# exp(c) of the last pair taken from exp(-c): a reciprocal on VectorE for one unit, a power of -1 on GpSimd for the other

## The chip, the core and the metric

One core of one Trainium2 chip runs the whole program. The metric is the device time of one execution in microseconds (us); less is better. The kernel before takes 178.74 us (median of two runs, 178.31 and 179.16).

## What is computed

A gated linear attention (4 batches, 8 heads, 768 steps, head size 48) feeds a two-layer network with a silu between:

```
f = 1 / (1 + exp(-f_logit))
for t in range(S):
    state = f[t] * state + outer(k[t], v[t])     # per batch and head, 48 x 48
    y[t]  = q[t] @ state
x   = y, heads side by side                       # 3072 tokens x 384
h   = x @ w_in                                    # 384 -> 2048
out = (h * sigmoid(h)) @ w_out                    # 2048 -> 384, float32
```

## The kernel before

The 768 steps of a batch are cut into chunks of 128. A unit is one chunk of one batch, with all 8 heads; two units make a pair, and 12 pairs make the program. Pairs 0 to 3 (form T) hold the first two chunks of one batch, pairs 4 to 11 (form N) the same chunk of two batches. Pair 10 is chunk 5 of batches 0 and 1, pair 11, the last, chunk 5 of batches 2 and 3. A unit is written (pair, place), so (11, 0) is batch 2 and (11, 1) batch 3; a step is written kind.pair.place.

The steps of a unit, with the lines that the profile shows for them:

- E and L (L229, L236; ScalarE): exp(-f) and ln(1 + that), the negative log of the gate. One pair's gates at a time.
- cs (L302; TensorE): running sum c of it over the chunk, by a triangular matrix, into PSUM.
- a and ia (both L307; ScalarE): a = exp(-c) and ia = exp(c), 128 x 384, from PSUM into buffers of the class x, of which there are five.
- qg and ki (both L312; VectorE or GpSimd): q * a and k * ia, into the two halves of a buffer qk.
- the transpose of qk: qkD (L327) is a transposing DMA that SyncE issues; it moves both halves at once, so it needs qg and ki.
- sc (L340; TensorE): scores; at (L344; VectorE): the mask, in two halves.
- vb (L180 on ScalarE, L182 on VectorE or GpSimd): v as bf16.
- y (L352 with the state of the chunk before, L356 with the masked scores and vb; TensorE), yc (a cast of y out of PSUM), and the transpose of y: yD (L368), a transposing DMA from SyncE, in the late pairs.
- d, sd, al, su (L373, L377, L309, L383): the state for the next chunk; su runs on GpSimd as two instructions.
- mi (L244; TensorE): 1st layer, eight steps of twelve matmuls a pair, over both units, so it needs both transposes of y; si (L249; ScalarE): silu; mo (L279; TensorE): 2nd layer; oc (L180 or L182): the copy out of PSUM; so (L287, L289): the store.

Nothing schedules at run time. A text, PLAN (lines 37 to 103), lists every step in one order, as `kind.pair.place:engine:slots`, with the engine (A ScalarE, V VectorE, G GpSimd, P TensorE, S SyncE) and the buffer slots. Each engine carries out its own steps strictly in that order and waits by semaphore for those of others. The loads (L223), the transposing DMAs and most stores are all issued by SyncE, in one queue. ScalarE has two sets of tables, one for exp and ln and one for silu; the program loads the other set (L473) at each turn from one kind to the other in PLAN. This is the stretch of it that the change touches (from lines 89 to 94, with the steps of TensorE, the masks but one entry and most steps of the two layers left out):

```
qg.10.1:G  q.11.0:S  qg.11.1:G  qg.10.0:V  so.7.1:S  sd.8.0:V
ia.11.1:A  a.11.0:A  qg.11.0:G  ia.11.0:A  qkD.10.1:S
ki.10.0:V  qkD.10.0:S  su.8.0:G  ki.11.0:G  oc.9.1:V  oc.9.0:A
v.10.0:S  v.11.0:S  ki.11.1:G  qkD.11.1:S  so.4.1:S
at.10.*:V  qkD.11.0:S  vb.10.1:A  vb.10.0:G  yD.10.1:S  yD.10.0:S
```

The step a.11.1 (exp(-c) of the other unit) stands earlier, on line 87. On TensorE the same stretch and what follows is: sc.10, the rest of mi.8, y.10.1, y.10.0, the last 28 matmuls of mo.8, sc.11, mi.10, y.11 and then mi, mo of pairs 10 and 11 to the end.

Of the kernel before, what the change touches and what calls it, by code (L numbers as in the profile page):

```python
# [10 lines left out]
F32 = mybir.dt.float32  # L11
# [18 lines left out]
    ('N', (0, 5), (1, 5)),  # L30
    ('N', (2, 5), (3, 5)),
]

SLOTS = dict(f=4, k=6, q=6, v=6, e=2, lf=3, x=5, qk=5, vb=7, qkT=4, qkTT=2, atm=4, yb=3, xT=4, hT=4, sd=2, al=6, ob=6, pb=8, st0=1, st1=1, st2=1, st3=1)

# [71 lines left out]
def kernel(  # L107
# [10 lines left out]
    nc = tc.nc  # L118
    B, H, S, D = q.shape
    C = 128  # L120
# [8 lines left out]
    sb = ctx.enter_context(tc.tile_pool(name="sb", bufs=1))  # L129
# [16 lines left out]
    triu = sb.tile([C, C], BF16, name="triu")  # L146
    ident = sb.tile([C, C], BF16, name="ident")
    ones = sb.tile([C, 1], BF16, name="ones")
    zero = sb.tile([C, 512], BF16, name="zero")
    two = any(kind == "T" for kind, *_ in PAIRS)  # L150
    if two:
# [11 lines left out]
    for word in PLAN.split():  # L163
        name, eng, got = word.split(":")
# [10 lines left out]
    at = lambda *key: where[key]  # L175
    ENG = {"A": nc.scalar, "V": nc.vector, "G": nc.gpsimd, "S": nc.sync}
# [20 lines left out]
    def emit(kind, rest, eng):  # L197
# [9 lines left out]
        P = rest[0]  # L207
# [65 lines left out]
        i = rest[1]  # L273
# [16 lines left out]
        elif kind == "cs":  # L290
            lf, cs = at("lf", P), at("cs", P, i)
            main = cs[:, 0:HD].rearrange("p (h d) -> p h d", d=D)
            if T:
                for j in range(2):
                    nc.tensor.matmul(main, tincl if j <= i else tstrict, lf[:, j, :, 0:D], start=(j == 0), stop=(j == 1), skip_group_check=True)  # L295
                if i == 1:
                    for p in range(NP):
                        for j in range(2):
                            nc.tensor.matmul(cs[:, HD + 2 * p:HD + 2 * p + 2], lf[:, j, 2 * p:2 * p + 2, :], halves,
                                             start=False, stop=(j == 1), skip_group_check=True)  # L300
            else:
                nc.tensor.matmul(main, triu, lf[:, i, :, 0:D], start=True, stop=True, skip_group_check=True)  # L302
                if not last:
                    for p in range(NP):
                        nc.tensor.matmul(cs[:, HD + p:HD + p + 1], lf[:, i, 2 * p:2 * p + 2, :], ones, start=False, stop=True, skip_group_check=True)
        elif kind in ("ia", "a"):
            nc.scalar.activation(at(kind, P, i).rearrange("p h d -> p (h d)"), at("cs", P, i)[:, 0:HD], AF.Exp, scale=1.0 if kind == "ia" else -1.0)  # L307
        elif kind == "al":
# [112 lines left out]
    def run(kind, rest, eng, got):  # L421
        if kind == "idle":
            for _ in range(rest[1]):
                nc.tensor.matmul(buf["pb", int(got)][:, 0:rest[0]], triu, zero[:, 0:rest[0]], start=True, stop=True, skip_group_check=True)  # L424
            return
        slots = iter(got.split(",") if got else [])
        for key in takes(kind, rest):
            if key not in where:
                cls = cls_of(key[0])
                if cls == "st":  # L430
                    cls = f"st{PAIRS[key[1]][1 + key[2]][0]}"
                elif cls == "qkT" and len(key) == 2:
                    cls = "qkTT"
                where[key] = buf[cls, int(next(slots))]
        assert next(slots, None) is None, (kind, rest, got)
        emit(kind, rest, eng)
# [4 lines left out]
    with tc.manual_schedule():  # L441
        nc.scalar.preload_act_table_set(TABLES["exp"])
        loads = [t for t in plan if t[0] in SRC][:4]
        for t in loads:
            run(*t)
        make_upper_triangular(nc, triu, 1.0, diag=True)
        nc.vector.memset(zero, 0.0)
        nc.vector.memset(ones, 1.0)
        if two:
            nc.gpsimd.memset(tincl, 0.0)  # L450
            nc.gpsimd.memset(tstrict, 0.0)
            for r in range(2):
                half = slice(r * HC, (r + 1) * HC)
                make_upper_triangular(nc, tincl[half, half], 1.0, diag=True)
                make_upper_triangular(nc, tstrict[half, half], 1.0, diag=False)
            nc.vector.memset(halves, 0.0)
            for r in range(2):
                nc.vector.memset(halves[r * HC:(r + 1) * HC, r:r + 1], 1.0)
        for cls in ("lf", "qk"):
            for s in range(SLOTS[cls]):  # L460
                nc.vector.memset(buf[cls, s][:, :, :, D:64], 0.0)
        make_identity(nc, ident)
        for b in range(B):
            nc.vector.memset(buf[f"st{b}", 0], 0.0)
        if two:
            for r in range(2):
                half = slice(r * HC, (r + 1) * HC)
                for j in range(2):
                    for t in range(2):
                        nc.vector.tensor_copy(masks[j][half, t * HC:(t + 1) * HC], (tincl if j <= t else tstrict)[half, half])  # L470
        for n, t in enumerate(plan):
            if n in turns:
                nc.scalar.preload_act_table_set(turns[n])  # L473
            if t not in loads:
                run(*t)
# [30 lines left out]
```

## Time and profile before

| | |
|---|---|
| median of two runs | 178.74 us |
| the profiled execution | 178.94 us |
| its span, first to last instruction | 177.2 us |
| granted TensorE clock, mean | 1.000 |
| ScalarE busy | 130.4 us (74%) |
| VectorE busy | 81.2 us (46%) |
| GpSimd busy | 62.5 us (35%) |

The profile is of one execution. PE is TensorE's matmuls, PEld its weight loads, DVE VectorE, ACT ScalarE, POOL GpSimd, SPq SyncE's queue. A timeline line reads: start, length, engine, line, operation, out<-in, count, and in brackets the idle time before it with what ended it; merged lines stand for several instructions in a row. The end of a matmul is modelled, so a line can overlap the next by some 0.17 us. The time from the issue of a DMA to its landing is counted from the start of the issue. Where an instruction waits for several things the profile names the one that ended last by its record, which need not be the one that it needed.

### The profile page before, as it was taken

Reading aid. Unit: us, or ns where it says so; the run is one execution under the profiler, and the core shown is the slowest. Engines: PE = TensorE matmul, PEld = TensorE weight load, DVE = VectorE, ACT = ScalarE, POOL = GpSimd, SP = SyncE. Lnnn points to the kernel's source line nnn. Section 1 sums busy time; section 2 is a strip of 40 time slices with the busy share of each in tenths; the row PEclk is TensorE's granted clock in tenths of the full one; section 3 lists DMA queues with packets and bytes.
Section 4 is the critical chain, followed back from the end, with each engine's and each line's share of the span. In section 5 each row is a group of like instructions: output and inputs, shape, how many; then the busy total and the mean of one; then the engine's idle time right before and its main releaser. Section 6 shows DMA issues by size and latency. Waiting matters only on the chain.

```text
span 177.2 us, 4721 instructions
## 1 busy us (share of the span) xinstructions
PE 170.6 (96%) x1912; PEld 124.7 (70%) x1915; DVE 81.2 (46%) x165; ACT 130.4 (74%) x241; POOL 62.5 (35%) x105
## 2 busy tenths in 40 slices
PE   6998999999999999999999999999999999999991
PEld 2446688666886788766787687686797686877860
DVE  7089751047795783125777174035770152520110
ACT  3968578953999989998499788899589574281721
POOL 6056593102383348400647323400471960000001
PEclk9999999999999999999999999999999999999999
DMA  5999999999999989997698796899968998132202
GB/s 145 301 311 256 213 225 204 188 179 237 218 196 201 211 177 199 219 204 151 135 231 152 148 228 141 213 192 212 234 129 191 212 150 242 48 91 87 93 0 89
DMA packets 110453, 32.12 MB, mean 181 GB/s; under 512 B 104080, under 2 KB 110256, under 8 KB 110432
## 3 DMA queue, kind: packets, MB, share of 16 engines
q1 hardware_dynamic: 106432, 27.89, 76.2%
q0 software_dynamic: 4000, 3.93, 12.2%
q8 instruction: 15, 0.25, 0.6%
q14 instruction: 6, 0.05, 0.1%
HBM read 25.17 MB, written 4.72 MB: 169 GB/s over the span
## 4 chain that ended last, share of the span: by engine, by line
PE 74%; ACT 9%; DVE 6%; DMA 4%; SPq 3%; issue 2%; DVEq 0%; ACTq 0%
PE pb L279 32%; PE pb L244 27%; DVE qk L312 3%; DMA q<-in_q_dram 3%; ACT hT L249 3%; PE pb L340 2%; ACT L473 2%; ACT x L307 2%; PE pb L352 2%; PE pb L356 2%; PE pb L336 1%; SPq L368 1%; DMA out_dram<-ob 1%; SPq L223 1%; PE pb L364 1%
## 5 line engine op out<-in xcount | busy, mean ns | idle before, releaser
L244 PE MATMUL pb<-xT,w_in_sb 128*128 128x256 bf16 x576 | 69.3, 272 | 0.5 <-ACT ob L180 0.2
L279 PE MATMUL pb<-w_out_sb,hT 128*128 128x384 bf16 x384 | 68.5, 326 | 0.0
L244 PEld LDWEIGHTS <-w_in_sb 128*128 128x128 bf16 x576 | 54.9, 98 | 9.6 <-issue 1.2
L249 ACT ACTIVATE hT<-pb 128x512 bf16<-128x512 f32 x96 | 50.5, 610 | 10.7 <-PE pb L244 10.5
L279 PEld LDWEIGHTS <-hT 128*128 128x128 bf16 x384 | 36.2, 98 | 21.0
L383 POOL TENSOR_TENSOR st<-sd,al 48x192 bf16<-48x192 f32 x40 | 21.7, 543 | 56.8 <-PE pb L352 34.2
L344 DVE TENSOR_TENSOR atm<-pb,triu 128x512 bf16<-128x512 f32 x32 | 20.1, 684 | 11.2 <-PE pb L340 6.6
L307 ACT ACTIVATE x<-pb 128x384 f32<-128x384 f32 x48 | 21.1, 497 | 5.2 <-PE pb L295 3.1
L473 ACT ACT_TABLE_LOAD x17 | 21.8, 1283 | 0.3
L182 DVE COPY ob<-pb 128x384 f32<-128x384 f32 x10 | 5.4, 552 | 26.6 <-PE pb L279 26.6
L377 DVE TENSOR_TENSOR sd<-pb,st 128x384 f32<-128x384 f32 x16 | 8.8, 553 | 11.8 <-PE pb L373 10.3
L312 POOL TENSOR_TENSOR qk<-k,x 128x384 bf16<-128x384 f32 x11 | 12.0, 1102 | 5.5 <-ACT x L307 2.4
L312 POOL TENSOR_TENSOR qk<-q,x 128x384 bf16<-128x384 f32 x11 | 10.9, 997 | 8.5 <-ACT x L307 5.5
L229 ACT ACTIVATE e<-f 128x768 f32<-128x768 f32 (+1 forms) x13 | 10.2, 792 | 4.8 <-DMA f<-in_f_logit_dram 4.8
L180 ACT COPY ob<-pb 128x384 f32<-128x384 f32 x14 | 6.7, 482 | 9.0 <-PE pb L279 8.2
L312 DVE TENSOR_TENSOR qk<-q,x 128x384 bf16<-128x384 f32 x13 | 8.6, 682 | 7.7 <-DMA q<-in_q_dram 4.2
L289 POOL DMA_DIRECT2D out_dram<-ob x3 | 1.7, 562 | 28.5 <-DVE ob L182 28.5
L424 PE MATMUL pb<-zero,triu 128*128 128x512 bf16 (+1 forms) x27 | 9.8, 463 | 1.5 <-POOL triu masks.py:66 1.4
L344 DVE TENSOR_TENSOR atm<-pb,mask 128x512 bf16<-128x512 f32 x16 | 10.2, 684 | 2.1 <-PE pb L336 1.0
L182 POOL CAST vb<-v 128x384 bf16<-128x384 f32 x12 | 6.5, 551 | 10.9 <-DMA v<-in_v_dram 10.5
L182 DVE CAST yb<-pb 128x384 bf16<-128x384 f32 x14 | 7.6, 555 | 5.4 <-PE pb L356 2.8
L180 ACT CAST yb<-pb 128x384 bf16<-128x384 f32 x10 | 4.8, 490 | 5.8 <-PE pb L356 4.3
(71 smaller groups left out, 148.8 us busy)
## 6 DMA issues: line engine op xcount, KB each, us to landing
f<-in_f_logit_dram SPq DMA_DIRECT2D x11, 384.0 KB, 5.2
k<-in_k_dram SPq DMA_DIRECT2D x10, 384.0 KB, 5.2
q<-in_q_dram SPq DMA_DIRECT2D x10, 384.0 KB, 5.4
v<-in_v_dram SPq DMA_DIRECT2D x10, 384.0 KB, 5.3
out_dram<-ob SPq DMA_DIRECT2D x13, 192.0 KB, 2.1
w_in_sb<-in_moe_w_in_dram POOLq DMA_DIRECT2D x4, 384.0 KB, 8.4
w_out_sb<-in_moe_w_out_dram POOLq DMA_DIRECT2D x4, 384.0 KB, 10.3
out_dram<-ob SPq DMA_DIRECT2D x14, 96.0 KB, 3.5
```

Source lines behind the costliest of these rows:

```text
L180: nc.scalar.copy(dst, src)
L182: ENG[eng].tensor_copy(dst, src)
L229: return nc.scalar.activation(e, at("f", P)[:, j * w:(j + 1) * w], AF.Exp, scale=-1.0)
L244: nc.tensor.matmul(h[:, i, cols], w_in_sb[:, kk, n * 128:(n + 1) * 128], at("xT", P)[:, kk, cols], start=(kk == 0), stop=(kk == KT - 1))
L249: return nc.scalar.activation(at("hT", P)[:, 2 * j:2 * j + 2, :], at("h", P, j).rearrange("p (n c) -> p n c", n=2), AF.Silu)
L279: nc.tensor.matmul(o, at("hT", P)[:, n, i * C:(i + 1) * C], w_out_sb[:, n, :], start=(n == 0), stop=(n == NT - 1))
L307: nc.scalar.activation(at(kind, P, i).rearrange("p h d -> p (h d)"), at("cs", P, i)[:, 0:HD], AF.Exp, scale=1.0 if kind == "ia" else -1.0)
L312: ENG[eng].tensor_mul(at("qk", P, i)[:, j, :, 0:D], heads("qk"[j], P, i), at("ia" if j else "a", P, i))
L344: ENG[eng].tensor_mul(at("atm", P, i)[:, r], at(f"s{r}", P, i).rearrange("p (n c) -> p n c", c=C), mask[:, None, :].to_broadcast([C, NP, C]))
L383: nc.gpsimd.tensor_mul(at("st", P, i)[lo:lo + D, :, r * D:(r + 1) * D], at("sd", P, i)[lo:lo + D, :, r * D:(r + 1) * D], al_of(P, i)[lo:lo ...
L424: nc.tensor.matmul(buf["pb", int(got)][:, 0:rest[0]], triu, zero[:, 0:rest[0]], start=True, stop=True, skip_group_check=True)
L473: nc.scalar.preload_act_table_set(turns[n])
```

## The change

For the last pair alone, ia no longer comes from the running sum by a second exp on ScalarE, but from a, its reciprocal. Unit (11, 0) takes `nc.vector.reciprocal`, unit (11, 1) an element-wise `pow` on GpSimd with a second operand of -1, a new tile of 128 x 1 that is read broadcast over the 384 columns. Both stand where ia.11.0 and ia.11.1 stood in PLAN, but now in the queues of VectorE and GpSimd; PLAN, its slots and the turns of the tables stay as they are. Results go to the same buffers in float32.

```diff
+TURNED_OVER = {(11, 0): 'reciprocal', (11, 1): 'G'}
...
+    minus = sb.tile([C, 1], F32, name="minus")
...
+        elif kind == "ia" and (P, i) in TURNED_OVER:
+            how = TURNED_OVER[P, i]
+            if how == "reciprocal":
+                nc.vector.reciprocal(at("ia", P, i), at("a", P, i))
+            else:
+                ENG[how].tensor_tensor(out=at("ia", P, i), in0=at("a", P, i), in1=minus[:, :, None].to_broadcast([C, H, D]), op=mybir.AluOpType.pow)
         elif kind in ("ia", "a"):
             nc.scalar.activation(at(kind, P, i).rearrange("p h d -> p (h d)"), at("cs", P, i)[:, 0:HD], AF.Exp, scale=1.0 if kind == "ia" else -1.0)
...
         nc.vector.memset(ones, 1.0)
+        nc.vector.memset(minus, -1.0)
```

The order on the two engines becomes: VectorE qg.10.0, sd.8.0, reciprocal, ki.10.0, oc.9.1, the masks of pair 10; GpSimd qg.10.1, qg.11.1, pow, qg.11.0, su.8.0 (two instructions), ki.11.0, ki.11.1, vb.10.0, the stores.

## The prediction

> **What bounds the kernel now.** I read the page's busy times first, then the chain of work that ended last in order of time, then the timeline of one engine after another around the change.
>
> ```profile
> PE   170.6 (96%) x1912; PEld 124.7 (70%) x1915; DVE 81.2 (46%) x165; ACT 130.4 (74%) x241; POOL 62.5 (35%) x105
> ```
> ```profile
> 136.97 0.44 PE pb L244 x4
> 137.41 3.25 PE pb L279 x20
> 140.66 1.31 PE pb L244 x12
> 141.97 0.55 PE pb L340 x16
> 142.52 2.75 PE pb L244 x24
> ...
> 146.46 0.20 PE pb L356 x8
> 146.66 4.55 PE pb L279 x28
> 151.21 0.55 PE pb L340 x16
> 151.76 1.43 PE pb L244 x12
> ...
> 173.58 0.48 ACT ob L180
> ```
>
> The first fence is the page's part 1 without its heading; the second is the chain in order of time (start, length, what). TensorE is busy for 96% of the span, and from 136.97 us to the end the chain is matmuls back to back, with one copy behind them. So in this stretch anything that makes TensorE wait is added to the time in full, and nothing that frees another engine is worth anything unless TensorE waited for it. Nothing later can win a wait back: there are no gaps in which to catch up.
>
> What feeds TensorE here comes from three in-order queues. First GpSimd (timeline; two answers, because the first names one instruction alone):
>
> ```profile
> 136.99 1.00 POOL L312 TENSOR_TENSOR qk<-q,x 128x384 bf16<-128x384 f32 x1 [3.59 <-ACT x L307]
> ```
> ```profile
> 137.94 1.00 POOL L312 TENSOR_TENSOR qk<-q,x 128x384 bf16<-128x384 f32 x1
> 138.90 1.08 POOL L383 TENSOR_TENSOR st<-sd,al 48x192 bf16<-48x192 f32 x2
> 140.06 1.95 POOL L312 TENSOR_TENSOR qk<-k,x 128x384 bf16<-128x384 f32 x2
> 141.96 0.50 POOL L182 CAST vb<-v 128x384 bf16<-128x384 f32 x1
> ```
>
> These are qg.11.1, qg.11.0, su.8.0, ki.11.0 with ki.11.1, and vb.10.0. GpSimd is idle for 3.59 us before qg.11.1, and that looks like room for the new work. It is not: the new step stands behind qg.11.1. The wait is put down to ScalarE, but qg.11.1 reads a.11.1, made long before; what it lacks is q of pair 11, and from qg.11.1 on GpSimd has no gap until vb.10.0 is done at 142.46. The load, and the rest of SyncE's queue (timeline, then the DMA view of single issues, whose last number is the time from issue to landing):
>
> ```profile
> 133.14 0.57 SPq L223 DMA_DIRECT2D q<-in_q_dram  x1
> 133.76 1.03 SPq L289 DMA_DIRECT2D out_dram<-ob  x1
> 134.90 2.70 SPq L327 DMA_TRANSPOSE qkT<-qk  x2
> 137.65 1.91 SPq L223 DMA_DIRECT2D v<-in_v_dram  x2
> 142.04 1.24 SPq L327 DMA_TRANSPOSE qkT<-qk  x1
> 143.32 1.28 SPq L289 DMA_DIRECT2D out_dram<-ob  x1
> 144.65 1.99 SPq L327 DMA_TRANSPOSE qkT<-qk  x1
> 146.91 2.84 SPq L368 DMA_TRANSPOSE xT<-yb  x2
> ```
> ```profile
> q<-in_q_dram SPq DMA_DIRECT2D x1, 384.0 KB, 3.7
> ```
> ```profile
> qkT<-qk SPq DMA_TRANSPOSE x1, 4.9
> ```
> ```profile
> xT<-yb SPq DMA_TRANSPOSE x1, 2.3
> ```
>
> q lands at 133.14 + 3.7 = 136.84, and qg.11.1 starts at 136.99. The transpose at 142.04 (qkD.11.1) leaves 0.03 us after the two ki end (140.06 + 1.95 = 142.01): it waits for GpSimd. The 4.9 us is that of the transpose at 144.65 (qkD.11.0), the 2.3 us that of the second one of yb (yD.10.0).
>
> **The change part by part.**
>
> *Two exps leave ScalarE.* They are two of these:
>
> ```profile
> 136.42 1.26 ACT L307 ACTIVATE x<-pb 128x384 f32<-128x384 f32 x3
> 139.40 0.48 ACT L180 COPY ob<-pb 128x384 f32<-128x384 f32 x1 [1.72 <-PE pb L279]
> ```
>
> ScalarE ends a little earlier and then waits for TensorE until 139.40 as before. Gain: nothing. The most that it could be if all of it lay on the path is two thirds of 1.26, 0.84 us. The table loads stay. What does move is a.11.0: it is the second of the three and becomes the first, done at about 136.9 (one takes 0.48).
>
> *The memset of -1* is one more instruction for VectorE, over one column, before the first load has landed; VectorE then idles until q is there. Nothing.
>
> *The reciprocal on VectorE.* Its price R is not in the trace, and it also brings a new wait: it needs a.11.0 (136.9), and ki.10.0, which ran long before, is now queued behind it.
>
> ```profile
> 131.04 0.55 DVE L312 TENSOR_TENSOR qk<-k,x 128x384 bf16<-128x384 f32 x1
> 140.75 0.56 DVE L182 COPY ob<-pb 128x384 f32<-128x384 f32 x1 [9.16 <-PE pb L279]
> ```
>
> The low end for R is one pass over this shape, 0.55 us (the multiply above). For the high end I take a division as eight such passes, 4.4 us, an estimate. I take 0.55, the nearest row of the same engine and shape. Then ki.10.0 ends at 136.95 + 0.55 + 0.55 = 138.05 instead of 131.59, and qkD.10.0, the second of the two transposes at 134.90, leaves at 138.1 instead of some 136.3. With its own landing time
>
> ```profile
> qkT<-qk SPq DMA_TRANSPOSE x1, 3.6
> ```
>
> it lands at 141.7; sc.10.0 is at 141.97 in the chain. So the move uses up 1.8 of 2.1 us of slack and costs nothing. Behind it in SyncE's queue the two loads of v move from 137.65 to about 139.5; with 4.2 us to landing v of pair 10 is there at 143.7, and its cast on GpSimd, with 0.50, would end at 144.2, before y.10.0 wants it (below). With R = 4.4 qkD.10.0 leaves at 141.95 and lands at 145.55: sc.10.0 would wait 3.6 us.
>
> ```profile
> v<-in_v_dram SPq DMA_DIRECT2D x1, 384.0 KB, 4.2
> ```
>
> By the Trainium skill, "VectorE: DVE Perf Modes", the walkthrough of the 8-slice pipeline, the reciprocal is an iterative divide with a repeat count of 8. At that page's 0.96 GHz and, as I read it, eight cycles an element, an estimate is 8 x 384 / 0.96 = 3.2 us; sc.10.0 would wait some 2.4 us, and the sum would be 181.4 us if the power cost nothing. No run here shows a reciprocal yet.
>
> *The power on GpSimd.* It starts when qg.11.1 is done, at 137.94, and takes X; all that GpSimd does after it comes X later, because there is no gap. No row shows a power. The low end is one pass with two operands, 1.00 us (the multiply above). For the high end: a power has to be put together from a logarithm, a product and an exponential, which I count as about twenty arithmetic steps (split off the exponent 3, polynomial 6, scale and round 4, polynomial 5, reassemble 2) and with special cases thirty; thirty passes at 1.00 us are 30 us. Steps kept in registers have no second operand to fetch; the nearest row for that is the cast, 0.50 us a pass. I take twenty at 0.50: X = 10 us, an estimate, and keep 1 to 30.
>
> Now along the path. (1) vb.10.0 ends at 142.46 + 10 = 152.46. TensorE wants it for y.10.0:
>
> ```profile
> 146.13 0.33 PE L352 MATMUL pb<-st,qkT 128*128 128x96 bf16 x4
> 146.30 0.36 PE L356 MATMUL pb<-vb,atm 128*128 128x48 bf16 x8
> ```
>
> at 146.30. That is X - 3.84 = 6.16 us of wait (su.8.0 holds the line above it until 149.98, inside the same wait). (2) The transposes of pair 11 need ki, so qkD.11.1 leaves at 152.04, and SyncE's queue behind it (a store, qkD.11.0, the two transposes of yb) moves as one block, X later. (3) qkD.11.0 lands at 144.65 + 4.9 + 10 = 159.55, where the chain has sc.11 at 151.21, its second half some 0.28 later: about X - 1.9 = 8.1. (4) yD.10.0, the second of the two yb transposes, leaves at 146.91 + 2.84 - 1.20 = 148.55 and lands 2.3 later, 150.85; plus 10 is 160.85. The next matmuls, mi.10.2, start at 151.69:
>
> ```profile
> 151.69 1.49 PE L244 MATMUL pb<-xT,w_in_sb 128*128 128x256 bf16 x12
> ```
>
> That is X - 0.84 = 9.2 us late, and this wait comes last, so it holds the others within it. If the transposes went through faster, being alone (issues of 1.24 and a store of 0.6, as elsewhere in the queue), it could come down to about 7; but the stores that GpSimd issues behind vb.10.0 move with them and crowd them as before. After that everything follows from TensorE.
>
> The reciprocal's shift lies inside this wait, whatever R is between its ends: qkD.11.1 at 152.04 comes after all that SyncE had to send. Sum: 0 + 0 + 0 + 9.2. The profiled execution took 178.94 (177.2 span and 1.7 around it; the median of the runs is 0.2 less): 188.1 us.
>
> **The rivals.**
>
> - *Not slower: the power is one pass or few.* Place: GpSimd behind qg.11.1; price 1 us; the point that decides: X = 0.84 for the first delay of TensorE by (4), and X about 4.4 for 2%. At X = 1 and R = 0.55 the time is 179.1. For it: the multiply of this shape takes 1.00 us. Against it: a power isn't one arithmetic step.
> - *Quick power, slow reciprocal.* VectorE becomes the cause: ki.10.0 late, sc.10.0 waits up to 3.6 us (R = 4.4): 182.5; with R about 3.2 it is 181.4.
> - *Long power.* X = 30: 178.94 + 29.2 = 208.1 us.
> - *TensorE slows down after the wait.* The first matmuls of the program:
>
> ```profile
> 1.37 4.66 PE L424 MATMUL pb<-zero,triu 128*128 128x512 bf16 x11 [1.37 <-POOL triu masks.py:66]
> 7.32 0.59 PE L424 MATMUL pb<-zero,triu 128*128 128x512 bf16 x2
> ```
>
> Eleven (ten of 512 columns, one of 256) take 4.66 us, 0.44 each; two later ones take 0.59 less the 0.17 of a modelled end, 0.21 each. So it starts at half pace, though the granted clock in the windows is 1.00 throughout. If an idle TensorE falls back to that, the 28 matmuls of mo.8 take 9.1 instead of 4.55: from 152.66 to 161.8, then sc.11 to 162.3, against 160.85 in (4): 1.5 us more, 189.6 us. For it: the wait before su.8.0 alone is 149.98 - 146.29 = 3.7 us. Against it: no row shows a slow matmul after a wait, as there is none this long. The Trainium skill, "TensorE: Matmul & The Clock Gate", Part 1, states that rule: half clock after an idle window of about 3.4 us. The slow start agrees with it; that it comes back is not shown here.
> - *The relief of ScalarE counts.* 178.1 us, if all of the 0.84 us were on the path. The chain holds no ScalarE piece between 136.97 and 173.5.
>
> **How the numbers follow.** The sum with X between 6 and 18 has 0.34 (its own range 184 to 196); the same with a slower TensorE 0.18; a long power, 18 us and over, 0.24 (a quarter of it over 30 us); a quick power with a slow reciprocal 0.10; both quick 0.12; the relief 0.02. I take 188.1 us. From 181 to 210 us only the last two and the power over some 31 us are left out, 0.12 + 0.02 + 0.06 = 0.20. A measurement of this kernel can tell about 2% (3.6 us) from no change. Slower than that: 0.34 + 0.18 + 0.24 = 0.76. Within: 0.12 + 0.10 + most of 0.02, 0.23. Faster: 0.01.
>
> **What would show it.** In the changed kernel's profile: a POOL row of the power between the two qg, starting near 138 us, its length X; then qg.11.0, su.8.0, ki and vb without gaps; TensorE waiting for POOL before y.10.0 by X - 3.84, and for a DMA into qkT or xT before sc.11 and mi.10; a DVE reciprocal starting at 136.9, right after ScalarE's exp, and no wait of TensorE at sc.10. The prediction fails by its size if X is far from 10; by its mechanism if GpSimd's rows behind the power do not move with it, if TensorE waits at sc.10 first (then R counts), or if the wait of TensorE is not the row's X less about 0.8.

## The result, and the profile after

The changed kernel takes 238.55 us (238.22 and 238.88) against 178.74 before: ratio 1.335, 95% interval 1.319 to 1.350. The forecast was 188.1 us, 181 to 210: the right direction, and far too small. The profiled execution took 238.88 us, its span is 237.1 against 177.2.

The profiled executions reach the stretch in question up to 6 us apart (133.0 to 139.2 us in the table below), though TensorE's steps up to there are the same in all these kernels, so profiles are compared from one matmul ahead of the change, cs.11.0, to the end. Its rows before and after, from TensorE's timelines (the kernel after has L305 for L302, as its lines are 3 to 10 further on):

```profile
133.82 0.33 PE L302 MATMUL pb<-lf,triu 128*128 128x384 bf16 x1
```
```profile
133.28 0.33 PE L305 MATMUL pb<-lf,triu 128*128 128x384 bf16 x1
142.64 0.62 PE L349 MATMUL pb<-qkT 48*128 48x128 bf16 x16 [1.21 <-DMA qkT<-qk]
...
146.64 0.36 PE L365 MATMUL pb<-vb,atm 128*128 128x48 bf16 x8
201.10 0.48 PE L361 MATMUL pb<-st,qkT 128*128 128x96 bf16 x4 [54.09 <-POOL st L392]
203.56 0.48 PE L365 MATMUL pb<-vb,atm 128*128 128x48 bf16 x8 [1.99 <-POOL vb L185]
203.87 6.17 PE L282 MATMUL pb<-w_out_sb,hT 128*128 128x384 bf16 x28
209.97 0.40 PE L349 MATMUL pb<-qkT 48*128 48x128 bf16 x8
211.00 0.40 PE L349 MATMUL pb<-qkT 48*128 48x128 bf16 x8 [0.63 <-DMA qkT<-qk]
211.63 1.47 PE L247 MATMUL pb<-xT,w_in_sb 128*128 128x256 bf16 x12 [0.23 <-DMA xT<-yb]
```

From cs.11.0 to the end: 177.2 - 133.82 = 43.4 us before, 237.1 - 133.28 = 103.8 after, 60.4 more. TensorE waits 1.2 us at sc.10, then 54.1 for su.8.0 and 2.0 for vb.10.0, both on GpSimd, then shortly for the transposes of qk and of y. What GpSimd did, in the chain that ended last (start, length, what):

```profile
137.47 61.56 POOL x L314
199.02 0.97 POOL qk L321
...
203.01 0.51 POOL vb L185
203.52 0.80 SPq L336
...
206.60 2.57 SPq L377
...
209.28 2.31 DMA xT<-yb
211.59 0.04 issue
211.63 1.47 PE pb L247 x12
```

One instruction, the power, takes 61.56 us, and everything of GpSimd follows it without a gap. Behind it the chain goes over SyncE's transposes to mi.10.2, as the prediction had it. TensorE waits 0.23 us there, right behind 0.63 us at sc.11 for a transpose of qk, so the two end close together. The engines' busy times and the slices of the page say the same from afar:

```profile
PE 172.7 (73%) x1915; PEld 125.4 (53%) x1915; DVE 84.0 (35%) x167; ACT 129.5 (55%) x239; POOL 123.5 (52%) x106
...
PEclk9999999999999999999999999855555555599999
```

GpSimd gains 61 us, TensorE 2. The granted clock of TensorE, 9 in every slice before, falls to 5 in the wait. VectorE and SyncE at the other end of the change:

```profile
136.40 2.55 DVE L312 RECIPROCAL x<-x 128x384 f32<-128x384 f32 x1 [5.82 <-ACT x L316]
138.87 0.49 DVE L321 TENSOR_TENSOR qk<-k,x 128x384 bf16<-128x384 f32 x1
```
```profile
134.62 6.00 SPq L336 DMA_TRANSPOSE qkT<-qk x2
140.68 2.24 SPq L226 DMA_DIRECT2D v<-in_v_dram x2
```

The reciprocal takes 2.55 us and starts on ScalarE's exp; ki.10.0 stands behind it, 9.3 us behind qg.10.0 where it was 0.9; its transpose ends the pair of issues late, and the two loads of v leave 7.4 us behind cs.11.0 instead of 3.8 (140.68 here, 137.65 before).

### The profile page after: what moved, and what is told of

It reads as the page before. It is cut to its first block, busy times and chain, and to the rows that moved or that the text cites. A ratio compares the mean times of both kernels' runs of the same rounds, so it can differ in the third digit from the quotient of the medians.

```text
span 237.1 us, 4727 instructions
## 1 busy us (share of the span) xinstructions
PE 172.7 (73%) x1915; PEld 125.4 (53%) x1915; DVE 84.0 (35%) x167; ACT 129.5 (55%) x239; POOL 123.5 (52%) x106
## 4 chain that ended last, share of the span: by engine, by line
PE 50%; POOL 27%; ACT 7%; DMA 5%; DVE 4%; SPq 3%; issue 2%; POOLq 0%; DVEq 0%; ACTq 0%
POOL x L314 26%; PE pb L282 21%; PE pb L247 18%; DMA q<-in_q_dram 4%; ACT hT L252 2%; DVE qk L321 2%; ACT L483 2%; ACT x L316 2%; SPq L377 1%; PE pb L349 1%; PE pb L361 1%; PE pb L365 1%; PE pb L345 1%; SPq L336 1%; DMA xT<-yb 1%
## 5 line engine op out<-in xcount | busy, mean ns | idle before, releaser
L282 PE MATMUL pb<-w_out_sb,hT 128*128 128x384 bf16 x384 | 70.0, 331 | 0.0
L314 POOL TENSOR_TENSOR x<-x,minus 128x384 f32<-128x384 f32 x1 | 61.6, 61557 | 0.0
L282 PEld LDWEIGHTS <-hT 128*128 128x128 bf16 x384 | 36.7, 99 | 22.1 <-issue 1.8
L361 PE MATMUL pb<-st,qkT 128*128 128x96 bf16 x64 | 5.5, 210 | 54.1 <-POOL st L392 54.1
L183 ACT CAST vb<-v 128x384 bf16<-128x384 f32 x6 | 3.2, 538 | 56.5 <-PE pb L365 56.5
L361 PEld LDWEIGHTS <-qkT 128*128 128x128 bf16 x64 | 4.3, 99 | 55.1 <-issue 54.2
L316 ACT ACTIVATE x<-pb 128x384 f32<-128x384 f32 x46 | 20.3, 498 | 5.5 <-PE pb L298 3.3
```

What stands on the lines that cost most here:

```text
L282: nc.tensor.matmul(o, at("hT", P)[:, n, i * C:(i + 1) * C], w_out_sb[:, n, :], start=(n == 0), stop=(n == NT - 1))
L314: ENG[how].tensor_tensor(out=at("ia", P, i), in0=at("a", P, i), in1=minus[:, :, None].to_broadcast([C, H, D]), op=mybir.AluOpType.pow)
L361: nc.tensor.matmul(y[:, 2 * D * p:2 * D * (p + 1)], qT, st[:, p, :], start=first, stop=T, skip_group_check=True)
```

## The experiments

Theory A: the power costs by the column whatever it computes, GpSimd's queue moves by that, and the reciprocal's own waits lie inside. Its rivals: a cost paid once (B), a cost that hangs on the data (C), or parts that add up. All runs of the table are profiles of one execution; the last column is what is more than in the kernel before.

| kernel | cs.11.0 | span | to the end | more |
|---|---|---|---|---|
| before | 133.82 | 177.2 | 43.4 | |
| after | 133.28 | 237.1 | 103.8 | 60.4 |
| pow_alone | 134.16 | 238.2 | 104.0 | 60.7 |
| pow_early | 133.68 | 233.3 | 99.6 | 56.2 |
| pow_warm | 137.51 | 243.5 | 106.0 | 62.6 |
| pow_1_head | 133.03 | 182.9 | 49.9 | 6.5 |
| mult_for_pow | 137.23 | 184.2 | 47.0 | 3.6 |
| recip_alone | 133.85 | 181.1 | 47.3 | 3.9 |
| recip_loads_first | 136.31 | 181.4 | 45.1 | 1.7 |
| recip_behind_ki | 136.28 | 179.6 | 43.3 | -0.1 |
| recip_both | 139.18 | 182.5 | 43.3 | -0.1 |

**prices.** The kernel before, with single instructions behind its end.

```diff
+        def pw(n, parts=C, base=a, e=minus, op=POW):
+            nc.gpsimd.tensor_tensor(out=j1[0:parts, 0:n], in0=base[0:parts, 0:n],
+                                    in1=e[0:parts, :, None].to_broadcast([parts, n, D]), op=op)
+        for n in (8, 8, 4, 2, 1):
+            pw(n)
...
+        for n in (8, 4, 2, 1):
+            nc.vector.reciprocal(j2[:, 0:n], a[:, 0:n])
```

> The kernel before with single instructions added behind its end: powers on GpSimd of 128 x 384 twice, then 192, 96 and 48 columns, then 384 columns on 32 and on 8 partitions, with a base of ones, with an exponent of 2, and a multiply; reciprocals on VectorE of 384, 192, 96 and 48 columns and a multiply. Only their rows count, not the time of the run. Theory A (the power costs by the column, some 160 ns each, 61.56 us / 384): 61.6, 61.6, 30.8, 15.4, 7.7 us; 61.6 on 32 partitions, as each group of partitions has its own core; the same with other data. Theory B (most of the 61.56 us is paid once, at the first use): about 61 for the first and few us for all others. Theory C (the cost hangs on the data): clearly less with a base of ones or an exponent of 2. The reciprocal of 384 columns: 2.55 us, and 1.3, 0.7, 0.4 for the shorter ones if it goes by the column.

Groups by form of GpSimd, from 174.6 to 297 us and from 300 us on, then of VectorE (count, then busy us and mean ns of one):

```profile
L485 POOL TENSOR_TENSOR x<-x,minus 128x384 f32<-128x384 f32 x2 | 123.1, 61551 | 0.1
```
```profile
L485 POOL TENSOR_TENSOR x<-x,two__2709 128x384 f32<-128x384 f32 x1 | 61.5, 61520 | 0.1
L485 POOL TENSOR_TENSOR x<-x,minus 32x384 f32<-32x384 f32 x1 | 61.5, 61507 | 0.1
L485 POOL TENSOR_TENSOR x<-x,minus 8x384 f32<-8x384 f32 x1 | 61.5, 61505 | 0.1
L485 POOL TENSOR_TENSOR x<-x,minus 128x192 f32<-128x192 f32 x1 | 30.9, 30916 | 0.1
L485 POOL TENSOR_TENSOR x<-x,minus 128x96 f32<-128x96 f32 x1 | 15.6, 15615 | 0.1
L485 POOL TENSOR_TENSOR x<-x,minus 128x48 f32<-128x48 f32 x1 | 8.0, 7997 | 0.1
```
```profile
L494 DVE RECIPROCAL x<-x 128x384 f32<-128x384 f32 x1 | 2.5, 2548 | 0.0
L494 DVE RECIPROCAL x<-x 128x192 f32<-128x192 f32 x1 | 1.4, 1353 | 0.0
L494 DVE RECIPROCAL x<-x 128x96 f32<-128x96 f32 x1 | 0.8, 753 | 0.0
L494 DVE RECIPROCAL x<-x 128x48 f32<-128x48 f32 x1 | 0.5, 453 | 0.0
```

The first power costs what the second does (61.58 us by its own row, so 61.52 for the other), so B falls. Exponent 2 costs the same, and so does a base of ones (61.52 us, one instruction that starts at 475.92), so C falls as far as these data go. Half the columns cost half: (61.52 - 30.92) us / 192 = 159 ns a column, with 0.3 us fixed. Eight partitions cost what 128 do. The multiply in the same form takes 0.82 us. The reciprocal costs (2548 - 1353) / 192 = 6.2 ns a column and some 0.15 us fixed. The Trainium skill, "VectorE: DVE Perf Modes", the walkthrough of the 8-slice pipeline, was read in the prediction as eight cycles a column, an estimate of 8.3 ns at its 0.96 GHz; the measured 6.2 ns decide.

**pow_1_head.** Of unit (11, 1) one head by the power, seven by the reciprocal, so that the power is about as long as had been forecast.

```diff
+                n = POW_HEADS    # 1
+                ENG[how].tensor_tensor(out=at("ia", P, i)[:, 0:n], ..., op=mybir.AluOpType.pow)
+                nc.vector.reciprocal(at("ia", P, i)[:, n:H], at("a", P, i)[:, n:H])
```

> The changed kernel, but for unit (11, 1) only one head of eight (48 of 384 columns) goes by the power, the other seven by a reciprocal on VectorE. Theory A: the power takes 7.7 us, and the prediction's path (late by the power less 0.84) gives 178.94 + 6.9 = 185.8 us, with the clock of TensorE at half only if its wait is over some 3.4 us (it is about 3.9). Theory B (paid once): some 237 us.

Ratio 1.040 (1.034 to 1.046), which is 186.2 us on the 178.98 of the kernel before in those runs, and 6.5 us more in the profile. From its timelines, GpSimd's power and TensorE behind it, and the windows (length; then each engine's busy time; then the granted clock, the DMA share and GB/s):

```profile
137.16 8.04 POOL L316 TENSOR_TENSOR x<-x,minus 128x48 f32<-128x48 f32 x1
```
```profile
147.27 0.33 PE L364 MATMUL pb<-st,qkT 128*128 128x96 bf16 x4 [0.52 <-POOL st L395]
149.74 0.48 PE L368 MATMUL pb<-vb,atm 128*128 128x48 bf16 x8 [2.13 <-POOL vb L186]
150.04 6.25 PE L283 MATMUL pb<-w_out_sb,hT 128*128 128x384 bf16 x28
```
```profile
150.00:153.00 3.00, 3.00 (x16) 1.44 (x13) 0.56 (x1) 0.51 (x1) 1.91 (x4) 0.50 0.89 189
```

The path of the prediction holds where its size does: its two ends, X less 3 and X less 0.84, give 5.0 and 7.2 us, and 6.5 came. The half clock is there too (0.50), after waits of 0.52 and 2.13 us with 0.33 us of work between them by its row. That is 2.65 us of waiting, not the 3.9 of the expectation, as TensorE had already waited 1.21 us at sc.10.

**pow_alone.** Only the power; unit (11, 0) keeps its exp.

```diff
-TURNED_OVER = {(11, 0): 'reciprocal', (11, 1): 'G'}
+TURNED_OVER = {(11, 1): 'G'}
```

> Only the power on GpSimd; unit (11, 0) keeps its exp on ScalarE. Theory A (the reciprocal's waits lie inside the power's): the time of the changed kernel, 238 to 239 us, TensorE's last wait ending at the same place. Rival (the two parts add up): 3.2 us less, 235.3 us.

Ratio 1.334 (1.324 to 1.343), 60.7 us more against 60.4 with both. The parts do not add up; the reciprocal is free beside the power. TensorE does not wait at sc.10 here. Its last wait is the one at sc.11, for a transpose of qk that lands 6.4 us after its issue, and mi.10 follows without one:

```profile
212.28 0.40 PE L349 MATMUL pb<-qkT 48*128 48x128 bf16 x8 [1.08 <-DMA qkT<-qk]
```

**pow_early.** The power one place earlier in GpSimd's queue.

```diff
-... qg.11.1:G:1 mi.9.5:P:6 ... ia.11.1:A:3 a.11.0:A:2 ...
+... ia.11.1:A:3 qg.11.1:G:1 mi.9.5:P:6 ... a.11.0:A:2 ...
```

> The changed kernel with the power one place earlier in GpSimd's queue, ahead of qg.11.1, and the turn of the tables kept where it was. Theory A (GpSimd's idle time before qg.11.1 could have been used, and all behind the power moves with it): the power starts 5.0 us earlier, at about 132.5, and qg.11.1 with its 0.95 comes behind it, so 4.0 us less: 234.5 us. Rival (something other than GpSimd's queue ends the wait): no change, 238.5 us.

Ratio 1.319 (1.307 to 1.331); in the profile 56.2 more instead of 60.4, so 4.2 us less, as expected. The two ratios alone do not show it, as their intervals overlap; the start of the power does, 4.9 us earlier than in the changed kernel when counted from cs.11.0. The idle time ahead of qg.11.1 can be used only by what stands ahead of it.

```profile
132.99 61.56 POOL L314 TENSOR_TENSOR x<-x,minus 128x384 f32<-128x384 f32 x1
```

**pow_warm.** TensorE kept busy while it waits.

```diff
-y.10.0:P:1 yc.10.0:V:1
+idle.512.245::1 y.10.0:P:1 yc.10.0:V:1
```

> The changed kernel with 245 matmuls of 512 zero columns ahead of y.10.0, so that TensorE is busy for some 53 us of its wait. Theory A (TensorE falls to half clock in the wait, which makes the 28 matmuls behind it 1.5 us longer, but the transposes of pair 11 and of y end later still): granted clock about 1.0 behind the wait, the 28 matmuls back at 4.7 us, the waits at sc.11 and mi.10 longer by as much, and the time unchanged, 238 to 239 us. Rival (the half clock is on the path): 1.5 us less, 237 us.

```profile
205.28 0.33 PE L361 MATMUL pb<-st,qkT 128*128 128x96 bf16 x4 [1.15 <-POOL st L392]
207.75 0.36 PE L365 MATMUL pb<-vb,atm 128*128 128x48 bf16 x8 [2.14 <-POOL vb L185]
207.95 4.71 PE L282 MATMUL pb<-w_out_sb,hT 128*128 128x384 bf16 x28
212.59 0.40 PE L349 MATMUL pb<-qkT 48*128 48x128 bf16 x8
216.14 0.61 PE L349 MATMUL pb<-qkT 48*128 48x128 bf16 x8 [3.15 <-DMA qkT<-qk]
216.68 2.74 PE L247 MATMUL pb<-xT,w_in_sb 128*128 128x256 bf16 x12
```

The rival falls: the 28 matmuls are 1.5 us faster (4.71), and nothing is gained, as sc.11 then waits 3.15 us for its transpose. "Unchanged" was wrong as well: by the profiles it is 2.2 us slower (62.6 more against 60.4; the ratio, 1.355 with 1.342 to 1.368, points the same way, but its interval touches that of the changed kernel). Of that 1.3 us is the half clock, which now comes after the wait of 3.15 us and falls on mi.10.2 (2.74 us for 1.47), where nothing hides it; the other 0.9 us is a later landing of the transpose in this one execution (6.9 us after its issue against 6.0 in the changed kernel), whose cause stays open.

**mult_for_pow.** A multiply in place of the power, so that -exp(-c) stands for exp(c) in unit (11, 1).

```diff
-op=mybir.AluOpType.pow)
+op=mybir.AluOpType.mult)
```

> The changed kernel with a multiply in place of the power, the same instruction otherwise, so that exp(c) of unit (11, 1) is replaced by -exp(-c): what the change would cost if a power were one pass of some 0.8 us. Prediction's rival (not slower): 179.1 us. Theory A (the reciprocal's waits, hidden behind the power until now, come out): late by 3.9 us as with the reciprocal alone, 182 to 183 us, counted from cs.11.0 to the end 47.2 us against 43.4 before.

Ratio 1.022 (1.003 to 1.040), 3.6 us more in the profile. With a power of 0.83 us the change would still have been slower by some 2%, by the reciprocal. TensorE waits 1.48, 0.83 and 1.06 us at sc.10, sc.11 and mi.10, the three places where the reciprocal alone makes it wait (below).

**recip_alone, recip_loads_first, recip_behind_ki, recip_both.** Only the reciprocal; the same with SyncE's loads of v ahead of the transpose of (10, 0); the same with the reciprocal behind ki.10.0; both units by reciprocals, (11, 1) ahead of ki.10.0 and (11, 0) behind it.

```diff
-TURNED_OVER = {(11, 0): 'reciprocal', (11, 1): 'G'}
+TURNED_OVER = {(11, 0): 'reciprocal'}
```
```diff
-mi.8.7:P:2 ki.10.0:V: qkD.10.0:S:1 ... v.10.0:S:2 v.11.0:S:0
+mi.8.7:P:2 ki.10.0:V: v.10.0:S:2 v.11.0:S:0 qkD.10.0:S:1 ...
```
```diff
-... a.11.0:A:2 qg.11.0:G:0 ia.11.0:A:4 ... ki.10.0:V: ...
+... a.11.0:A:2 qg.11.0:G:0 ... ki.10.0:V: ia.11.0:A:4 ...
```

> Only the reciprocal on VectorE; unit (11, 1) keeps its exp on ScalarE. Theory A (ki.10.0 is queued behind the reciprocal, and sc.10.0 waits for its transpose): TensorE waits about 1.2 us at sc.10, as it did in the changed kernel, and nothing wins it back: 179.9 to 180.2 us, ratio 1.006 to 1.008. Rival (the prediction's price of one pass, or slack takes it up): no wait at sc.10, ratio 1.000.

> The reciprocal alone, with the two loads of v moved ahead of the transpose of unit (10, 0) in SyncE's queue; nothing else. Theory A: the 3.2 us that the reciprocal alone costs are two waits, 1.84 us at sc.10 (its transpose issued late behind ki.10.0) and 0.97 + 0.84 us at sc.11 and mi.10 (the loads of v, queued behind that transpose, land 4 us late and crowd the transposes of pair 11). With the loads ahead only the first stays: ratio about 1.010, 180.8 us. Rival (the late part comes from sc.10 alone): 1.020 again.

> As the one before, but the reciprocal stands behind ki.10.0 in VectorE's queue. Theory A (what costs is the order, not the 2.55 us themselves): ki.10.0 is back at 131, no wait at sc.10, ki.11.0 on GpSimd still finds its factor (reciprocal done at about 139, ki.11.0 at 140): ratio 1.000. Rival (the 2.55 us cost wherever they stand): the same as in the run before, 1.006 to 1.008.

> Both units by a reciprocal on VectorE, with no power: the one for (11, 1) ahead of ki.10.0, where its input is long there, the one for (11, 0) behind ki.10.0. ScalarE loses its two exps. Theory A (nothing waits for these exps, and two reciprocals of 2.55 us fit into VectorE's idle time if nothing is queued behind them): if the first one, 5 us after qg.10.0, moves ki.10.0 by no more than 2 us, ratio 1.000 to 1.003. Rival (the relief of ScalarE is worth something): 0.995 or less. Rival (2.55 us ahead of ki.10.0 already use up its slack): 1.005 or more.

Ratios: 1.020 (1.018 to 1.022), 1.017 (1.008 to 1.026), 1.002 (0.998 to 1.006) and 0.998 (0.990 to 1.006). The first was more than expected, three times the wait at sc.10 that had been seen. SyncE's queue with the reciprocal alone, and TensorE's waits (us in all, times, longest) with it and with the loads first:

```profile
135.19 6.62 SPq L336 DMA_TRANSPOSE qkT<-qk x2
141.86 2.37 SPq L226 DMA_DIRECT2D v<-in_v_dram x2
144.33 3.63 SPq L336 DMA_TRANSPOSE qkT<-qk x1
```
```profile
PE pb L349 <- DMA qkT<-qk: 2.8, 2, 1.8
PE pb L247 <- DMA xT<-yb: 0.8, 1, 0.8
```
```profile
PE pb L349 <- DMA qkT<-qk: 1.7, 1, 1.7
```

The late ki.10.0 costs twice: 1.8 us at sc.10, and, since the loads of v queue behind its transpose and then crowd the transposes of pair 11 (the issue at 144.33 alone takes 3.63 us against 1.24), 1.8 us more at sc.11 and mi.10. With the loads ahead the second part is gone from the waits, and 1.7 of 3.9 us stay; the two ratios alone do not tell these apart, as their intervals overlap. With the reciprocal behind ki.10.0 nothing is left, at the same 2.55 us:

```profile
139.78 2.55 DVE L312 RECIPROCAL x<-x 128x384 f32<-128x384 f32 x1 [5.73 <-ACT x L316]
```

In recip_both the reciprocal ahead of ki.10.0 has its input early, and ki.10.0 starts 5.5 us behind qg.10.0 instead of 0.9. That is more than the 2 us that the expectation allowed, and TensorE still has no wait. In recip_alone, behind a reciprocal with a late input, it starts 9.7 us behind, and that is too late. With both by reciprocals the two exps have left ScalarE and nothing is gained: no version here beats the kernel before.

## Why the prediction was wrong, step by step

- *The power's size (the step that failed).* "I take twenty at 0.50: X = 10 us, and keep 1 to 30." It takes 61.56 us, 62 times the multiply that bounded it from below and twice the upper end. Counting arithmetic steps and pricing each as a pass was no bound: nothing in the trace tied a power to such steps, and it was the one term that the whole sum hung on. In place of twenty passes the runs show 159 ns a column, whatever the partitions and the data tried (prices). What the instruction does in that time stays open.
- *Where it stands, and what moves with it.* Right: it starts when qg.11.1 is done (137.47), and GpSimd follows without gaps. pow_early shows that the queue, not the input, sets its start.
- *The path, X less 0.84.* Right in size, somewhat high: with 61.56 it gives 60.7, and 60.4 (both) and 60.7 (power alone) came; with 8.04 us 7.2, and 6.5 came. With the right X the forecast would have been 178.94 + 60.7 = 239.7 us for 238.88 measured. Which transpose ends last is less certain than the prediction had it: yD.10.0 at mi.10 in the changed kernel, by 0.23 us, but qkD.11.0 at sc.11 in pow_alone. One sign that the prediction had named for a wrong mechanism did come, a wait at sc.10 first (1.21 us); pow_alone, without that wait and as long, shows that it did not set the time.
- *The reciprocal.* Taken at 0.55 us, it takes 2.55, between the ends given. That it costs nothing held only inside the power's wait (pow_alone). By itself it costs 3.9 us. The prediction's own formula with 2.55 us gives sc.10 a wait of 1.7; 1.84 came with the reciprocal alone and 1.21 in the changed kernel; what it left out, in the rival too, is the second half, by the loads of v behind that transpose.
- *ScalarE's relief and the memset.* Nothing, as said (recip_both).
- *The rival of not slower.* It was priced with a reciprocal of 0.55 us. With the measured one even a power of one pass is 3.6 us slower (mult_for_pow). That is the size of the rival of a quick power with a slow reciprocal, 181.4 to 182.5 us, though by waits at sc.10, sc.11 and mi.10 and not at sc.10 alone.
- *The rival of a slower TensorE.* The half clock is real, and its 1.5 us were not on the path: the 28 matmuls took 6.17 instead of 4.71 us, not 9.1, as the full clock came back on the way, and they ended before the transposes had landed. In pow_warm they were back at 4.71 without a gain.

## What to carry to other kernels

An operation that no row of the trace shows should be run by itself before its cost is argued: here one instruction of the same shape and engine cost 62 times its neighbour. Idle time of an in-order engine is no room for a step that stands behind the instruction that waits; and a step that waits for a late input also holds the step behind it, here ki.10.0, whose transposing DMA held two loads in turn. Placed behind ki.10.0, the same reciprocal was free.

## What the runs showed of the hardware

- The power on GpSimd: 159 ns a column (float32, 128 partitions), the same time for 8 partitions, for a base of ones and for an exponent of 2, and on its first use; the multiply in the same form took 0.82 us for 384 columns.
- TensorE's clock: 0.50 behind the waits of 54 us, of 3.15 us (pow_warm), and of 0.52 and 2.13 us (pow_1_head). Behind the waits of 1.15 and 2.14 us in pow_warm it was still 1.00, and the 28 matmuls took 4.71 us, though these waits are longer than those of pow_1_head. So the length of the waits alone does not settle it, and what does stays open. Inside the long wait it fell 5.2 us after the last matmul in the changed kernel and 3.0 us after it in pow_alone. It came back after some 3.3 us of work, from 203.56 to about 206.9 (windows of the changed kernel):

```profile
201.00:206.00 5.00, 2.92 (x19) 1.64 (x19) 0.56 (x1) 0.51 (x1) 4.67 (x8) 0.50 0.38 72
206.00:207.00 1.00, 1.00 (x5) 0.49 (x4) 0.00 (x0) 0.00 (x0) 0.00 (x0) 0.57 0.95 283
207.00:211.60 4.60, 3.77 (x35) 2.16 (x34) 1.14 (x2) 0.89 (x2) 0.00 (x0) 1.00 0.90 188
```

The Trainium skill, "TensorE: Matmul & The Clock Gate", Part 1, gives an idle window of about 3.4 us for the fall to half and a like one of work for the return. The return agrees (3.3 us); the fall came after less idle time than that in pow_1_head (0.52 and 2.13 us) and in pow_warm (3.15 us).
